# A retention and low-rank mixer kernel on one core: three of batch 0's v loads issued by GpSimd's queue, and the first batch's ramp in another order

## The chip, the cores and the metric

The kernel runs on one core of one Trainium2 chip. The metric is the device time of one execution in microseconds. A core has five engines that run side by side, each with its own queue of instructions, which it works off strictly in order: TensorE (PE in the profile, its weight loads PEld), VectorE (DVE), ScalarE (ACT), GpSimd (POOL) and SyncE (SP). They wait for one another through semaphores. Transfers between the chip's memory and the core's are issued from an engine's queue and then run by themselves; in this kernel SP issues most of them, and GpSimd those of the weights.

## The reference, cut to what matters

Batch, heads, tokens and head size are 4, 8, 768 and 64, so a token has 512 channels; the hidden size is 2048 and the rank 32.

```python
state = gamma * state + k_t (outer) v_t        # per head, gamma = 1 - 2^(-5-h)
y_t   = scale * q_t @ state                    # 768 tokens in order
x     = y laid out as (batch, 768, 512)
u     = x + (x^T @ U @ V)^T                    # low rank, over the tokens
out   = u + relu(u @ w_ch1) @ w_ch2
```

The kernel does the recurrence in six chunks of 128 tokens: inside a chunk by a masked product of q and k, across chunks by a state that goes on from chunk to chunk.

## The kernel before

The work is one long stream of matmuls, batch after batch. While a batch's MLP runs, the retention of the next batch is put in between the MLP's matmuls by a table (`PLANS`): each entry gives the number of the MLP slot ahead of which a step of the next batch stands. A slot is one group of MLP matmuls. Nothing is scheduled by the machine: the order in which the Python code calls the steps is the order in each engine's queue.

Batch 0 has no MLP ahead of it. Its retention, its low-rank part and the first load of weights are the *ramp*, and its order is written out by hand: a list of pairs of function and arguments, which a loop calls one after another. The change is in this list. The functions it names, all for batch 0:

- `run_idle(n, bank)`: n matmuls on zeros that only keep TensorE busy.
- `qd(i, e, engine)` and `kd(c, engine)`: scale half e of q's pair i (chunks 2i and 2i+1, whose tokens alternate between the halves), or k of chunk c, by the decay, into tile `qk`. G is GpSimd, V is DVE, A is ACT.
- `turn_q`, `turn_k`: four matmuls each with the identity, which transpose them; `evict_q`, `evict_k` copy the result from PSUM to `q0T` and `kT`.
- `scores(c)`, `keep(c, e)`: the products of q and k, and DVE's masking of them into tile `a`.
- `cast_v(c, engine)`: v to bf16 (`vb`). Chunk 5's is done in two halves.
- `sums(c)`, `state(c, engine)`: the sum of k and v over the chunks so far, in one PSUM bank, and its copy `st`, block by block. `sums` of a chunk writes to the bank that `state` of the chunk before read.
- `inter(c)`, `intra(c)`, `evict_x(c)`: the output of chunk c from the earlier chunks' state and from its own scores, and its copy `x`. Chunk 5 is done in two halves.
- `turn_x`, `low`, `evict_P`, `high`, `evict_u`: x transposed, the low-rank products and the eviction of their sum u to `uT`, which the MLP reads. `spread_V`, `evict_V` spread the matrix V.
- `load_w1(lo, w)`: a load of w columns of the first weight, issued by GpSimd.

Input tiles are loaded by `load_pair` (two chunks in 512 KB, into tile `in`) and `load_one` (one chunk in 256 KB, into `k_n` or `v_n`). SP's queue issues them at the program's start in this order: q of pair 0, k of chunks 0 and 1, q of pair 1, k 2, k 3, v of chunks 0 and 1, q of pair 2, k 4, v 2, k 5, v 3, v 4, v 5. In the order listings `DMA v_n_2 ... 128x8x64` is the load of v of chunk 2: 128 tokens, 8 heads, 64 elements.

Of the kernel before, what the change touches and what calls it, by code (L numbers as in the profile page):

```python
# [47 lines left out]
def kernel(  # L48
# [80 lines left out]

    gate = (1, 0)  # L130

    def load_one(t, b, c, src, nm):
# [3 lines left out]
        nc.sync.dma_start(out=n, in_=src[b, :, ts(c, P), :].rearrange("h p d -> p h d"))
# [181 lines left out]

    def kd(c, eng):
        t = qk_of(c)[:, 1]  # L320
        i, g = (in0[:, 0, :, c], Gk0) if c < 2 else (t0["k_n", c], Gk)
        eng.tensor_tensor(t, i, g[:, c].unsqueeze(2).to_broadcast([P, H, D]), op=ALU.mult)
# [488 lines left out]
    for f, *args in (
        (run_idle, 6, 5), (qd, 0, 1, V), (kd, 2, G), (run_idle, 11, 5), (qd, 0, 0, V), (qd, 1, 0, G),
        (kd, 0, V), (turn_k, 0), (turn_q, 0, 1), (turn_q, 0, 0), (kd, 1, V), (evict_k, 0, V),
        (evict_q, 0, 0, A), (run_idle, 1, 5), (evict_q, 0, 1, A), (turn_k, 1), (evict_k, 1, A),
        (scores, 1), (qd, 1, 1, V), (keep, 1, 0), (run_idle, 2, 2), (kd, 3, G), (scores, 0),
        (turn_q, 1, 1), (keep, 1, 1), (spread_V, 1), (turn_q, 1, 0), (evict_q, 1, 1, A), (keep, 0, 0),
        (evict_q, 1, 0, A), (keep, 0, 1), (cast_v, 1, V), (turn_k, 2), (qd, 2, 1, G), (evict_k, 2, A),
        (cast_v, 0, A), (spread_V, 0), (scores, 2), (kd, 4, G), (run_idle, 1, 1), (evict_V, 1, V),
        (keep, 2, 0), (turn_k, 3), (evict_V, 0, A), (sums, 0), (kd, 5, G), (evict_k, 3, A), (intra, 0),
        (state, 0, A), (keep, 2, 1), (scores, 3), (sums, 1), (qd, 2, 0, V), (run_idle, 1, 1),  # L820
        (keep, 3, 1), (load_w1, 0, 256), (evict_x, 0, A), (turn_q, 2, 1), (inter, 1), (state, 1, A),
        (keep, 3, 0), (turn_q, 2, 0), (turn_k, 4), (evict_q, 2, 1, A), (evict_k, 4, V), (intra, 1),
        (evict_q, 2, 0, A), (cast_v, 2, V), (scores, 4), (evict_x, 1, A), (sums, 2), (inter, 2),
        (intra, 2), (run_idle, 1, 0), (keep, 4, 1), (state, 2, A), (cast_v, 3, V),
        (load_w1, DH // 2, 256), (keep, 4, 0), (inter, 3), (turn_k, 5), (evict_x, 2, A), (intra, 3),
        (turn_x, 0, 0), (sums, 3), (evict_k, 5, A), (turn_x, 0, 2), (cast_v, 5, G, 0), (state, 3, V),
        (turn_x, 0, 1), (scores, 5), (cast_v, 5, G, 1), (cast_v, 4, A), (keep, 5, 0), (evict_x, 3, A),
        (sums, 4), (state, 4, A), (inter, 4), (intra, 4), (low, (0, 1, 2, 3)), (keep, 5, 1),
        (load_w1, 256, 768), (inter, 5, 0), (inter, 5, 1), (evict_x, 4, A), (intra, 5, 1),
        (intra, 5, 0), (turn_x, 0, 3), (evict_x, 5, V, 1), (low, (4,)), (evict_x, 5, A, 0),  # L830
        (low, (5,)), (turn_x, 1, 1), (turn_x, 1, 2), (evict_P, 0, A), (evict_P, 1, A), (turn_x, 1, 0),
        (high, 0, 0), (high, 0, 1), (high, 0, 3), (high, 1, 2), (evict_u, 0, 1, V), (high, 0, 2),
        (evict_u, 0, 3, A), (high, 1, 1), (high, 1, 0), (evict_u, 1, 2, V), (turn_x, 1, 3),
        (load_w1, DH // 2 + 256, 256), (evict_u, 0, 0, A), (high, 1, 3), (evict_u, 1, 0, V),
        (evict_u, 0, 2, A), (evict_u, 1, 1, V), (evict_u, 1, 3, A),
    ):
# [3 lines left out]
    PLANS = (  # L840
        {
            "in": [38, 41, 42, 46, 49, 52],
            "v": [47, 49, 57, 55, 58, 63],
            "T": [45, 49, 51, 54, 55, 63],
            "S": [((0,), 47), ((1,), 52), ((2,), 55), ((3,), 58), ((4,), 62), ((5,), 65)],
            "O": [49, 54, 57, 60, 64, 68],
            "load": [],
            "P": 69,
# [14 lines left out]
        {
            "in": [1, 8, 13, 14, 20, 23],
            "v": [27, 28, 33, 43, 39, 45],
            "T": [3, 13, 18, 18, 21, 26],
            "S": [((0, 1), 27), ((2,), 35), ((3,), 42), ((4,), 44), ((5,), 47)],
            "O": [31, 37, 43, 45, 50, 52],
            "load": [(3, 3, 0), (3, 4, 11), (3, 5, 14)],
            "P": 54,  # L870
            "n": [(0, 56), (1, 56), (2, 56), (3, 59), (4, 59), (5, 59)],
            "u": [],
        },
    )
# [1 line left out]
    for b in range(B):  # L876
        nxt = b + 1 < B
        slots = mlp1_slots(b)
        n1 = len(slots)
        side = {}  # L880
        set_banks([0, 1, 2, SA, SB, OB])
        if b == 0:
            taken.update({i: n for n, i in enumerate((1, 2, 0, OB, SA, SB, TP))})
# [9 lines left out]
            for j, i in enumerate([0, 5, 12, 14, 19, 24]):  # L893
# [1 line left out]
            for i, f, *args in ((8, g_sums, 0, 0, 2), (18, g_sums, 0, 2, 2), (23, w2_sum, 0, range(4)),
                                (26, g_sums, 0, 4, 2), (24, w2_sum, 1, (0,)), (28, w2_sum, 1, (1,)),
                                (33, g_sums, 0, 6, 1, range(3)), (32, w2_sum, 1, (2,)),
                                (33, g_sums, 0, 7, 1, range(3)), (33, hold_pool),
                                (39, w2_sum, 1, (3,)), (33, g_sums, 0, 6, 2, (3,))):
# [1 line left out]
            put(side, n1 + 22, flush)
        if b == 1:
            put(side, 21, flush)
# [1 line left out]
            for j, i in enumerate([9, 0, 4]):
                put(side, i, lambda j=j: mix_r(1, j))
        if b:
            for m0, w, i in zip((0, 2, 4, 6, 7), (2, 2, 2, 1, 1), [[12, 20, 25, 30, 32], [12, 16, 25, 28, 32], [12, 20, 25, 29, 32]][b - 1]):
# [54 lines left out]
```

## Time and profile before

| what | us |
|---|---|
| runs shown | 223.07, 223.14, 222.38; median 223.07 |
| the profiled execution, its own time | 222.57 |
| its span, first to last instruction | 220.8 |
| TensorE busy | 211.3 |
| DVE, ACT, GpSimd busy | 146.1, 121.4, 77.7 |
| first matmul of batch 0's MLP | 29.47 |

A row of the timeline reads: start, duration, engine, line, operation, what it writes `<-` what it reads, shape, count, and in brackets the idle time of the engine before it with what ended it. `SPq` is an issue of a transfer in SP's queue. A row on a transfer gives its count, its size and the median time from the issue's start to the landing. Most matmuls are recorded by one helper and so carry one line, L116; they are told apart by the tiles that they read: `<-q0T,kT` are scores, `<-vb,qk` sums, `<-st,q0T` inter, `<-vb,a` intra, `<-ident,qk` turns of q or k, `<-ident,x` turn_x, `<-x,Ub` low, `<-Vb,P_sb` high, `<-uT,w1b` the MLP.

### The profile page before, as it was taken

The numbers are of one execution on the slowest core, as the hardware profiler recorded it, in microseconds if no ns is written. First come the engines' busy times: TensorE is split into PE (matmuls) and PEld (weight loads), VectorE is DVE, ScalarE is ACT, GpSimd is POOL, SyncE is SP. The second block draws the span as 40 slices with busy tenths as digits, with TensorE's granted clock in tenths as the row PEclk, the third lists the DMA queues.
The fourth block names the chain that finished last, engine by engine and source line by source line (L and its number), as shares of the span: only waits on it lengthen the run. The fifth ranks groups of instructions, "written<-read, shape, count | busy, mean of one in ns | idle before, by whom it ended". The sixth has DMA issues, their size and how long they took to land.

```text
span 220.8 us, 5024 instructions
## 1 busy us (share of the span) xinstructions
PE 211.3 (96%) x1999; PEld 154.8 (70%) x2002; DVE 146.1 (66%) x293; ACT 121.4 (55%) x252; POOL 77.7 (35%) x89
## 2 busy tenths in 40 slices
PE   7868999999999999999999999999999999999993
PEld 2447755668888765667887876666887866668883
DVE  7678566798887872579974720889885602566662
ACT  3268856775147466777444737777444557771000
POOL 5075820004986501904243279550423430000000
PEclk9999999999999999999999999999999999999999
DMA  6999999999999968999999389999020570000222
GB/s 164 241 268 180 141 200 214 213 222 221 202 215 181 228 172 164 190 204 299 203 199 219 73 146 225 229 227 155 3 95 3 129 198 11 0 0 0 98 95 97
DMA packets 98583, 34.89 MB, mean 158 GB/s; under 512 B 86752, under 2 KB 94848, under 8 KB 98560
## 3 DMA queue, kind: packets, MB, share of 16 engines
q1 hardware_dynamic: 94112, 30.02, 66.5%
q0 software_dynamic: 4304, 4.29, 12.1%
q8 instruction: 15, 0.25, 0.5%
q10 hardware_dynamic: 144, 0.26, 0.3%
q14 instruction: 8, 0.07, 0.1%
HBM read 27.46 MB, written 6.29 MB: 153 GB/s over the span
## 4 chain that ended last, share of the span: by engine, by line
PE 88%; DVE 5%; ACT 4%; issue 1%; DVEq 0%; ACTq 0%
PE bk L116 86%; ACT st L310 1%; DVE a L463 1%; PE bk L440 1%; ACT q0T L310 1%; DVE gs L621 1%; DVE a L368 1%; ACT kT L310 1%; ACT P_sb L121 1%; DVE res L697 0%; DVE st L400 0%; PE bk L334 0%; ACT gT L121 0%; DVE Vb L312 0%; PE bk L346 0%
## 5 line engine op out<-in xcount | busy, mean ns | idle before, releaser
L116 PE MATMUL bk<-uT,w1b 128*128 128x384 bf16 x512 | 85.9, 326 | 0.0
L116 PEld LDWEIGHTS <-w1b 128*128 128x128 bf16 x512 | 53.7, 106 | 29.6 <-issue 0.4
L121 ACT ACTIVATE gT<-bk 128x384 bf16<-128x384 f32 x125 | 61.1, 490 | 23.8 <-PE bk L116 23.0
L697 DVE TENSOR_TENSOR res<-bk,res 128x256 f32<-128x256 f32 (+2 forms) x66 | 30.3, 462 | 21.3 <-PE bk L116 20.3
L116 PEld LDWEIGHTS <-gT 128*128 128x128 bf16 x384 | 36.3, 98 | 7.4 <-issue 1.8
L116 PE MATMUL bk<-w2b,gT 128*128 128x256 bf16 x288 | 37.6, 273 | 0.0
L116 PEld LDWEIGHTS <-gs 128*128 128x128 bf16 x296 | 27.5, 98 | 4.0
L268 POOL TENSOR_TENSOR qk<-k_n,Gk 128x512 bf16<-128x512 f32 x18 | 19.8, 1102 | 25.8 <-DMA k_n<-in_k_dram 19.2
L621 DVE TENSOR_TENSOR gs<-gT 128x768 bf16<-128x768 bf16 (+1 forms) x20 | 10.6, 532 | 27.4 <-ACT gT L121 27.4
L116 PE MATMUL bk<-w2s,gs 128*128 128x256 bf16 x192 | 25.7, 273 | 0.0
L463 DVE TENSOR_TENSOR a<-bk,mask 128x512 bf16<-128x512 f32 x36 | 22.9, 681 | 1.2 <-PE bk L116 1.0
L562 DVE TENSOR_TENSOR res<-bk,x 128x512 f32<-128x512 f32 x24 | 15.9, 687 | 9.3 <-PE bk L116 7.9
L697 POOL TENSOR_TENSOR res<-s,res 128x512 f32<-128x512 f32 (+2 forms) x13 | 13.7, 1059 | 22.6 <-DVE res L697 17.1
L480 ACT ACTIVATE x<-bk 128x512 bf16<-128x512 f32 x18 | 10.8, 598 | 18.7 <-PE bk L116 16.4
L273 POOL TENSOR_TENSOR qk<-q_n,Gq 128x512 bf16<-128x512 f32 x18 | 19.7, 1096 | 0.4 <-DMA q_n<-in_q_dram 0.2
L697 POOL TENSOR_TENSOR res<-c,res 128x256 f32<-128x256 f32 x12 | 8.7, 725 | 16.4 <-ACT c L692 16.4
L279 ACT ACTIVATE vb<-v_n 128x512 bf16<-128x512 f32 x18 | 11.0, 624 | 4.6 <-DMA v_n<-in_v_dram 4.5
L116 PE MATMUL bk<-w2b,gs 128*128 128x256 bf16 (+1 forms) x104 | 13.1, 265 | 0.0
L116 PE MATMUL bk<-w2s,gT 128*128 128x256 bf16 x96 | 13.1, 273 | 0.0
L621 DVE TENSOR_TENSOR gT<-gT 128x768 bf16<-128x768 bf16 (+1 forms) x20 | 12.0, 598 | 0.0
L567 ACT ACTIVATE x<-res 128x512 bf16<-128x512 f32 x15 | 9.1, 629 | 4.5 <-DVE res L562 4.5
L621 DVE TENSOR_TENSOR gs<-gs,gT 128x768 bf16<-128x768 bf16 (+1 forms) x20 | 11.1, 553 | 0.7
(98 smaller groups left out, 218.3 us busy)
## 6 DMA issues: line engine op xcount, KB each, us to landing
k_n<-in_k_dram SPq DMA_DIRECT2D x22, 256.0 KB, 4.8
v_n<-in_v_dram SPq DMA_DIRECT2D x22, 256.0 KB, 5.0
out_dram<-res SPq DMA_DIRECT2D x22, 256.0 KB, 2.5
q_n<-in_q_dram SPq DMA_DIRECT2D x18, 256.0 KB, 4.9
w2b<-in_moe_w_ch_dram POOLq DMA_DIRECT2D x4, 512.0 KB, 14.7
in<-in_q_dram SPq DMA_DIRECT2D x3, 512.0 KB, 6.2
w1b<-in_moe_w_ch_dram POOLq DMA_DIRECT2D x3, 256.0 KB, 6.1
...
```

The source lines that it names most:

```text
L116: nc.tensor.matmul(o, l, r, **kw)
L121: nc.scalar.activation(o, i, AF.Relu if relu else AF.Copy)
L268: eng.tensor_tensor(kd, k_n, Gk[:, c].unsqueeze(2).to_broadcast([P, H, D]), op=ALU.mult)
L273: eng.tensor_tensor(qd, rc[b, c]["q_n"], Gq[:, c].unsqueeze(2).to_broadcast([P, H, D]), op=ALU.mult)
L279: nc.scalar.activation(vb, rc[b, c]["v_n"], AF.Copy)
L310: nc.scalar.activation(o, i, AF.Copy)
L463: nc.vector.tensor_tensor(r["a"][:, e], r["s"][e].rearrange("p (n t) -> p n t", n=NP), mask4, op=ALU.mult)
L480: nc.scalar.activation(x_of(b, c), o, AF.Copy)
L562: nc.vector.tensor_tensor(res_of(b, j), h, xs[b, j], op=ALU.add)
L567: nc.scalar.activation(xs[b, j], res_of(b, j), AF.Copy)
L621: nc.vector.tensor_tensor(o, x, y, op=op)
L697: eng.tensor_tensor(x, y, x, op=ALU.add)
```

## The change

Three loads, v of chunks 2, 4 and 5, leave SP's queue. They are now issued by GpSimd's, from the middle of the ramp, by a new function `load_late`. Of SP's list there remains k 5 directly behind k 4, and then v 3. The ramp's list has another order, with other engines for some steps: q and k of pair 0 and q of pair 1 are divided between DVE and GpSimd, q's turns come ahead of k's, k 1 ahead of k 0. There are 20 idle matmuls in the list instead of 23. The two wide w1 loads of the ramp stand at its end. In `PLANS` and in the tables of side steps some slots are moved, mostly by one to three.

```diff
-    def load_one(t, b, c, src, nm):
+    def load_one(t, b, c, src, nm, eng=nc.sync):
...
-        nc.sync.dma_start(out=n, in_=src[b, :, ts(c, P), :].rearrange("h p d -> p h d"))
+        eng.dma_start(out=n, in_=src[b, :, ts(c, P), :].rearrange("h p d -> p h d"))
...
-    for what in ("q0", "kA", "q1", "k2", "k3", "vA", "q2", "k4", "v2", "k5", "v3", "v4", "v5"):
+    for what in ("q0", "kA", "q1", "k2", "k3", "vA", "q2", "k4", "k5", "v3"):
...
+    def load_late(nm, c, eng):
+        load_one(t0, 0, c, {"k": k, "v": v}[nm], nm + "_n", eng)
...
-        (run_idle, 6, 5), (qd, 0, 1, V), (kd, 2, G), (run_idle, 11, 5), (qd, 0, 0, V), (qd, 1, 0, G),
-        (kd, 0, V), (turn_k, 0), (turn_q, 0, 1), (turn_q, 0, 0), (kd, 1, V), (evict_k, 0, V),
...
+        (qd, 0, 0, V), (qd, 0, 1, G), (run_idle, 9, 5), (turn_q, 0, 1), (turn_q, 0, 0), (kd, 1, V),
+        (evict_q, 0, 0, A), (run_idle, 4, 5), (turn_k, 1), (evict_k, 1, A), (kd, 0, G),
...
+        (keep, 1, 0), (kd, 3, G), (load_late, "v", 2, G), (load_late, "v", 4, G),
+        (load_late, "v", 5, G), (keep, 1, 1), (evict_q, 1, 0, A), (turn_q, 1, 1),
...
-            "load": [(3, 0, 26), (3, 1, 42), (3, 2, 40), (2, 3, 4), (2, 4, 8), (2, 5, 17)],
+            "load": [(3, 0, 29), (3, 1, 43), (3, 2, 38), (2, 3, 5), (2, 4, 8), (2, 5, 17)],
```

GpSimd's queue from its first scaling to the first loads of the first weight, before:

```order
L322 TENSOR_TENSOR qk_2_201<-k_n_2_101,Gk 128x512
L327 TENSOR_TENSOR qk_2_201<-in_97,Gq_168 128x512
L322 TENSOR_TENSOR qk_3_267<-k_n_3_103,Gk 128x512
L327 TENSOR_TENSOR qk_5_317<-in_97,Gq_168 128x512
L322 TENSOR_TENSOR qk_4_336<-k_n_4_107,Gk 128x512
L322 TENSOR_TENSOR qk_5_317<-k_n_5_111,Gk 128x512
L161 DMA w1b_403<-in_moe_w_ch_dram 128x4x256
L161 DMA w1b_489<-in_moe_w_ch_dram 128x4x256
```

The same place of the changed kernel:

```order
L330 TENSOR_TENSOR qk_1_188<-in_97,Gq_162 128x512
L325 TENSOR_TENSOR qk_0_186<-in_97,Gk_164 128x512
L330 TENSOR_TENSOR qk_2_254<-in_97,Gq_162 128x512
L325 TENSOR_TENSOR qk_2_254<-k_n_2_101,Gk 128x512
L325 TENSOR_TENSOR qk_3_252<-k_n_3_103,Gk 128x512
L136 DMA v_n_2_287<-in_v_dram 128x8x64
L136 DMA v_n_4_289<-in_v_dram 128x8x64
L136 DMA v_n_5_291<-in_v_dram 128x8x64
L330 TENSOR_TENSOR qk_5_303<-in_97,Gq_162 128x512
L325 TENSOR_TENSOR qk_4_328<-k_n_4_107,Gk 128x512
L325 TENSOR_TENSOR qk_5_303<-k_n_5_109,Gk 128x512
L161 DMA w1b_428<-in_moe_w_ch_dram 128x4x256
```

Two scalings of pair 0 came in at the front, and the three loads of v stand between k of chunk 3 and q of chunk 5.

DVE's queue from the second masking of chunk 2 to v of chunk 2, before:

```order
L368 TENSOR_TENSOR a_2_327<-bk_20_326,mask 128x512
L327 TENSOR_TENSOR qk_4_336<-in_97,Gq_168 128x512
L368 TENSOR_TENSOR a_3_382<-bk_26_381,mask 128x512
L368 TENSOR_TENSOR a_3_382<-bk_25_380,mask 128x512
L312 COPY kT_4_431<-bk_31_425 128x512
L312 CAST vb_2_450<-v_n_2_109 128x512
L368 TENSOR_TENSOR a_4_454<-bk_33_453,mask 128x512
```

The same place of the changed kernel, from the masking of chunk 2's second half on, and on to the state of chunk 3:

```order
L371 TENSOR_TENSOR a_2_332<-bk_22_331,mask 128x512
L330 TENSOR_TENSOR qk_4_328<-in_97,Gq_162 128x512
L371 TENSOR_TENSOR a_3_381<-bk_26_379,mask 128x512
L371 TENSOR_TENSOR a_3_381<-bk_27_380,mask 128x512
L312 CAST x_1_443<-bk_28_400 128x512
L312 COPY kT_4_445<-bk_30_432 128x512
L312 CAST vb_2_455<-v_n_2_287 128x512
L371 TENSOR_TENSOR a_4_466<-bk_35_465,mask 128x512
L312 CAST vb_3_504<-v_n_3_111 128x512
L371 TENSOR_TENSOR a_4_466<-bk_34_464,mask 128x512
L403 TENSOR_TENSOR st_179<-bk_24_349,bmask 128x512
```

The output x of chunk 1 is now copied by DVE and stands ahead of k of chunk 4, and v of chunk 3 is cast between the two maskings of chunk 4.

More of the change, by code (lines that the diff above doesn't have):

```diff
@@ L817 @@
[L817 to L833, printed above, removed]
@@ L834 @@
-        (load_w1, DH // 2 + 256, 256), (evict_u, 0, 0, A), (high, 1, 3), (evict_u, 1, 0, V),
-        (evict_u, 0, 2, A), (evict_u, 1, 1, V), (evict_u, 1, 3, A),
+        (qd, 0, 0, V), (qd, 0, 1, G), (run_idle, 9, 5), (turn_q, 0, 1), (turn_q, 0, 0), (kd, 1, V),
+        (evict_q, 0, 0, A), (run_idle, 4, 5), (turn_k, 1), (evict_k, 1, A), (kd, 0, G),
+        (turn_k, 0), (evict_q, 0, 1, V), (run_idle, 1, 5), (scores, 1), (qd, 1, 1, V),
+        (qd, 1, 0, G), (run_idle, 1, 2), (turn_q, 1, 0), (evict_k, 0, A), (scores, 0), (kd, 2, G),
@@ new lines @@
+        (keep, 1, 0), (kd, 3, G), (load_late, "v", 2, G), (load_late, "v", 4, G),
+        (load_late, "v", 5, G), (keep, 1, 1), (evict_q, 1, 0, A), (turn_q, 1, 1),
+        (evict_q, 1, 1, A), (keep, 0, 1), (keep, 0, 0), (qd, 2, 1, G), (spread_V, 0),
+        (spread_V, 1), (evict_V, 1, A), (turn_k, 2), (evict_k, 2, V), (run_idle, 2, 1),
+        (turn_k, 3), (evict_k, 3, V), (evict_V, 0, A), (kd, 4, G), (scores, 2), (cast_v, 1, V),
+        (kd, 5, G), (cast_v, 0, A), (run_idle, 2, 1), (sums, 0), (keep, 2, 0), (state, 0, A),
@@ new lines @@
+        (intra, 0), (keep, 2, 1), (scores, 3), (evict_x, 0, A), (sums, 1), (inter, 1), (intra, 1),
+        (qd, 2, 0, V), (turn_q, 2, 1), (keep, 3, 0), (load_w1, 0, 256), (load_w1, DH // 2, 256),
+        (turn_k, 4), (turn_q, 2, 0), (keep, 3, 1), (evict_x, 1, V), (evict_k, 4, V), (state, 1, A),
+        (inter, 2), (evict_q, 2, 1, A), (cast_v, 2, V), (run_idle, 1, 0), (sums, 2),
+        (evict_q, 2, 0, A), (scores, 4), (intra, 2), (state, 2, A), (inter, 3), (evict_x, 2, A),
+        (turn_k, 5), (keep, 4, 1), (evict_k, 5, A), (turn_x, 0, 0), (cast_v, 3, V), (sums, 3),
@@ new lines @@
+        (keep, 4, 0), (intra, 3), (scores, 5), (turn_x, 0, 2), (state, 3, V), (cast_v, 4, A),
+        (keep, 5, 1), (evict_x, 3, A), (sums, 4), (state, 4, A), (keep, 5, 0), (inter, 4),
+        (intra, 4), (low, (0, 1, 2, 3)), (inter, 5, 1), (cast_v, 5, G, 1), (cast_v, 5, G, 0),
+        (intra, 5, 1), (evict_x, 5, V, 1), (evict_x, 4, A), (inter, 5, 0), (intra, 5, 0),
+        (turn_x, 0, 3), (turn_x, 0, 1), (low, (4,)), (evict_x, 5, A, 0), (low, (5,)),
+        (evict_P, 0, A), (turn_x, 1, 1), (turn_x, 1, 2), (turn_x, 1, 0), (evict_P, 1, A),
@@ L836 @@
+        (high, 0, 0), (high, 0, 1), (evict_u, 0, 0, V), (evict_u, 0, 1, V), (high, 1, 0),
+        (evict_u, 1, 0, A), (high, 0, 2), (turn_x, 1, 3), (high, 1, 2), (high, 0, 3),
+        (evict_u, 0, 2, V), (evict_u, 0, 3, V), (high, 1, 1), (evict_u, 1, 1, V), (high, 1, 3),
+        (evict_u, 1, 3, A), (evict_u, 1, 2, V), (load_w1, 256, 768),
+        (load_w1, DH // 2 + 256, 256),
     ):
@@ L841 @@
         {
[L842 to L843 removed]
+            "in": [38, 41, 44, 47, 52, 54],
+            "v": [47, 49, 56, 56, 59, 64],
             "T": [45, 49, 51, 54, 55, 63],
[L845 removed]
+            "S": [((0,), 47), ((1,), 52), ((2,), 55), ((3,), 57), ((4,), 62), ((5,), 65)],
             "O": [49, 54, 57, 60, 64, 68],
@@ L864 @@
             "in": [1, 8, 13, 14, 20, 23],
[L865 to L869, printed above, removed]
+            "v": [25, 28, 35, 40, 35, 41],
+            "T": [3, 12, 18, 16, 20, 26],
+            "S": [((0, 1), 27), ((2,), 37), ((3,), 42), ((4,), 45), ((5,), 47)],
+            "O": [32, 37, 43, 45, 50, 53],
+            "load": [(3, 3, 1), (3, 4, 9), (3, 5, 12)],
             "P": 54,
-            "n": [(0, 56), (1, 56), (2, 56), (3, 59), (4, 59), (5, 59)],
+            "n": [(0, 57), (1, 56), (2, 56), (3, 59), (4, 59), (5, 59)],
             "u": [],
@@ L892 @@
                 put(side, 14, lambda c=c, nm=nm: load_chunk(1, c, nm))
[L893 removed]
+            for j, i in enumerate([0, 5, 13, 15, 16, 24]):
                 put(side, i, lambda j=j: mix_r(0, j))
[L895 removed]
+            for i, f, *args in ((9, g_sums, 0, 0, 2), (17, g_sums, 0, 2, 2), (23, w2_sum, 0, range(4)),
                                 (26, g_sums, 0, 4, 2), (24, w2_sum, 1, (0,)), (28, w2_sum, 1, (1,)),
[L897 removed]
+                                (31, g_sums, 0, 6, 1, range(3)), (32, w2_sum, 1, (2,)),
                                 (33, g_sums, 0, 7, 1, range(3)), (33, hold_pool),
[L899 removed]
+                                (38, w2_sum, 1, (3,)), (34, g_sums, 0, 6, 2, (3,))):
                 put(side, i, lambda f=f, args=args: f(*args))
[L901 removed]
+            put(side, n1 + 23, flush)
         if b == 1:
[L903 removed]
+            put(side, 24, flush)
             slots[:2] = [lambda: mlp1_two(1, (0, HM), 0), lambda: None]
[L905 removed]
+            for j, i in enumerate([8, 0, 3]):
                 put(side, i, lambda j=j: mix_r(1, j))
         if b:
[L908 removed]
+            for m0, w, i in zip((0, 2, 4, 6, 7), (2, 2, 2, 1, 1), [[12, 22, 25, 30, 32], [12, 16, 25, 28, 33], [12, 20, 25, 28, 32]][b - 1]):
                 put(side, i, lambda m0=m0, w=w: g_sums(b, m0, w))
```

11 lines of the change are left out of this document (4 added, 7 removed).

## The prediction

> **What bounds the kernel now.** I read the page first, then the busy time by stretch, then the waits of TensorE, and last the rows of the ramp engine by engine.
>
> ```profile
> span 220.8 us, 5024 instructions
> PE 211.3 (96%) x1999; PEld 154.8 (70%) x2002; DVE 146.1 (66%) x293; ACT 121.4 (55%) x252; POOL 77.7 (35%) x89
> PE 88%; DVE 5%; ACT 4%; issue 1%; DVEq 0%; ACTq 0%
> ...
> 10.00:15.00 5.00, 2.84 (x51) 1.51 (x49) 3.31 (x7) 3.01 (x6) 3.04 (x3) 1.00 1.19 267
> 15.00:20.00 5.00, 4.35 (x84) 3.57 (x85) 4.53 (x7) 4.68 (x11) 2.08 (x2) 1.00 1.14 191
> 20.00:25.00 5.00, 3.93 (x81) 3.43 (x79) 3.39 (x8) 4.13 (x10) 3.84 (x6) 1.00 0.95 164
> 29.47:40.00 10.53, 10.53 (x65) 6.26 (x64) 6.38 (x12) 6.65 (x17) 0.00 (x0) 1.00 1.21 210
> ...
> PE bk L116 <- DVE a L463: 0.3, 1, 0.3
> ```
>
> TensorE is busy 96% of the span, and the chain that ended last is 88% TensorE. In the rows by stretch (first PE, then PEld, DVE, ACT, POOL, granted clock, DMA share, GB/s) it has no hole from 29.47 on; the last line is the only wait that the trace shows behind that point. So what stands behind 29.47, where the first matmul of batch 0's MLP begins, moves as a block: the change is worth what it moves that matmul by. In the ramp before it TensorE waits, and its turns are these:
>
> ```profile
> 11.63 0.42 PE L116 MATMUL bk<-q0T,kT 64*64 64x128 bf16 x16 [1.42 <-ACT kT L310]
> 19.27 0.39 PE L334 MATMUL bk<-ident,qk 128*128 128x128 bf16 x4
> 19.59 0.64 PE L116 MATMUL bk<-vb,a 64*128 64x64 bf16 x16
> 20.98 0.40 PE L116 MATMUL bk<-vb,qk 128*128 128x128 bf16 x4
> 23.16 0.39 PE L116 MATMUL bk<-vb,qk 128*128 128x128 bf16 x4
> 26.57 0.59 PE L116 MATMUL bk<-x,Ub 128*32 128x512 bf16 x2
> 29.47 3.41 PE L116 MATMUL bk<-uT,w1b 128*128 128x384 bf16 x20
> ```
>
> In the names of the table these are scores of chunk 1, turn_k 4, intra 1, sums 2, sums 3, low 4 and 5, and the first MLP slot. From sums 3 to the end of low 5 is 23.16 to 27.16, 4.0 us: the states of chunks 3 and 4 and the output of chunk 5 follow one another there. From low 5 to the MLP is 2.3 us more.
>
> The loads feed this:
>
> ```profile
> 11.83 1.68 SPq L136 DMA_DIRECT2D v_n<-in_v_dram  x1
> 13.55 1.85 SPq L136 DMA_DIRECT2D k_n<-in_k_dram  x1
> 15.45 4.76 SPq L136 DMA_DIRECT2D v_n<-in_v_dram  x3
> ...
> 16.00:18.00 2.00, 1.76 (x40) 1.50 (x39) 2.00 (x3) 1.79 (x5) 1.81 (x2) 1.00 1.33 223
> 18.00:20.00 2.00, 2.00 (x39) 1.69 (x37) 2.00 (x4) 1.89 (x5) 0.00 (x0) 1.00 0.84 142
> 20.00:22.00 2.00, 1.41 (x32) 1.21 (x30) 1.36 (x4) 1.54 (x5) 1.45 (x2) 1.00 0.84 189
> 22.00:24.00 2.00, 1.69 (x35) 1.57 (x36) 1.03 (x3) 1.90 (x5) 1.39 (x3) 1.00 0.89 136
> ...
> v_n<-in_v_dram SPq DMA_DIRECT2D x1, 256.0 KB, 7.6
> k_n<-in_k_dram SPq DMA_DIRECT2D x1, 256.0 KB, 6.9
> ...
> 20.55 1.04 POOL L322 TENSOR_TENSOR qk<-k_n,Gk 128x512 bf16<-128x512 f32 x1 [2.60 <-DMA k_n<-in_k_dram]
> 23.77 0.74 POOL L312 CAST vb<-v_n 128x256 bf16<-128x256 f32 x2 [0.61 <-DMA v_n<-in_v_dram]
> ```
>
> SP's queue issues v of chunk 2 at 11.83 (lands 7.6 later, 19.4), k of 5 at 13.55 (6.9 later, 20.45), then v of 3, 4 and 5; the three take 4.76 us to issue. GpSimd waits 2.60 us for k of 5, and v of 5 ends its wait at 23.77. The last column shows the transfers at 223 GB/s up to 18 and at 142, 189 and 136 after it: SP's issuing, not the transfer rate, thins out the last loads.
>
> **The change part by part.**
>
> *Front of the ramp.* Before, DVE made both q of pair 0 and both k; now each pair is divided between DVE and GpSimd, q is turned first, and k of chunk 1 ahead of k of 0. Prices of one scaling:
>
> ```profile
> 7.50 1.29 DVE L322 TENSOR_TENSOR qk<-in,Gk 128x512 bf16<-128x512 f32 x2 [0.80 <-DMA in<-in_k_dram]
> 17.05 1.46 DVE L327 TENSOR_TENSOR qk<-in,Gq 128x512 bf16<-128x512 f32 x1
> ...
> 16.92 1.04 POOL L322 TENSOR_TENSOR qk<-k_n,Gk 128x512 bf16<-128x512 f32 x1
> ```
>
> A DVE scaling is 0.65, but 1.46 where it starts beside one of GpSimd's (17.05 against 16.92). So I take the pairs as one behind the other: k of 1 is ready at 8.2 if DVE is first, at 9.0 if GpSimd is. Its turn (about 0.4 with the hand-over) and its eviction (0.6) put scores 1 at 9.3 to 10.3 instead of 11.63: 1.3 to 2.3 us ahead. Three idle matmuls fewer cost and save nothing, since they fill waits. That lead runs down to intra 1 (about 17.5 for 19.59), but behind it the PE queue holds turn_k 4 and sums 2, which hang on GpSimd and on loads. So the front alone is costed at nothing; if the loads came earlier, it would show.
>
> *GpSimd's queue.* It gains three issues between k of 3 and q of 5, and two scalings at the front. The price of an issue of 1024 pieces (128x8x64) is not in the trace from this engine. Nearest rows:
>
> ```profile
> 1.41 0.70 POOL L209 DMA_DIRECT2D Vs<-in_moe_V_dram  x1
> 2.10 0.88 POOL L210 DMA_DIRECT2D Ub<-in_moe_U_dram  x1
> ```
>
> Vs is 32 rows in 0.70, Ub 768 pieces (128x6x32) in 0.88; drawn on to 1024 that is 0.95, my value. Lower end 0.70; upper end SP's 1.68 for the same load. K of 3 ended before at about 14.1 behind two other scalings; one of these (1.03) is gone from ahead of it, so the issues start at 13.0 to 13.5. Three of 0.95 end at 16.2; q of 5 then ends at 17.2 and k of 4 at 18.3, so turn_k 4 comes at 18.4 against 19.27. The cover here is 0.9 us. At more than 1.25 us an issue it is used up.
>
> *The loads.* SP's order is the same up to k of 4. Then k of 5 has the place of v 2 (19.4, before 20.45) and v of 3 that of k 5 (20.45, before 21.55). GpSimd's loads run beside them:
>
> ```profile
> Vs<-in_moe_V_dram POOLq DMA_DIRECT2D x1, 48.0 KB, 5.7
> Ub<-in_moe_U_dram POOLq DMA_DIRECT2D x1, 48.0 KB, 6.6
> w1b<-in_moe_w_ch_dram POOLq DMA_DIRECT2D x2, 256.0 KB, 6.1
> v_n<-in_v_dram SPq DMA_DIRECT2D x1, 256.0 KB, 4.5
> ```
>
> From that queue, beside SP's traffic, 5.7 to 6.6 us pass to landing. V of 2, issued at 13.3, lands at 19.0 to 19.9 (before 19.4): no loss, no gain. V of 4 and 5 follow at 20.5 to 21.9, before 22.8 (by its place) and 23.7. The three take 768 KB of transfer time from SP's last two loads: at 223 GB/s 1.1 us for each 256 KB, of which I charge one to v of 3. So it lands at 21.5, as before, and k of 5 at 19.4 to 20.4.
>
> [...]
>
> *The path to the end.* V of 2 cast (0.42) at 19.5 to 20.4 lets sums 2 run at about 20.1, before 20.98. Then the state of 2 (0.78) to 21.1, inter 3, turn_k 5, the first turn_x (0.65 together) to 21.75. V of 3, landed at 21.5 and cast, lets sums 3 run at 22.0; before 23.16.
>
> ```profile
> 24.86 0.78 ACT L310 ACTIVATE st<-bk 64x256 bf16<-64x256 f32 x2 [0.31 <-PE bk L116]
> 14.49 0.42 DVE L312 CAST vb<-in 128x512 bf16<-128x512 f32 x1
> ```
>
> The 4.0 us behind sums 3 hold the same states, casts and outputs in nearly the same order; DVE's state of 3 now stands behind keep 4, so I add 0.15. Low 5 ends at 26.15 against 27.16: 1.0 us gained. The end of the ramp then has the same three turns, eight high products and one more turn; four of the first evictions on DVE feed the first MLP slot, which needs only two of them at its start. Costed at nothing; the other order of evictions could cost or give 0.2.
>
> *Weights and later slots.* The first two w1 loads are issued when k of 5 is done, about 20.5 (before 21.54, 6.1 to landing): at the MLP by 27. The 768 wide load stands behind the cast of v 5, which is earlier too. The moved slots of batches 1 and 2 lie where TensorE has work queued: nothing, with 0.4 us either way as bounds, from the one 0.3 us wait.
>
> Sum: 1.0 us. The profiled execution took 222.57 (span 220.8 and 1.8 around it), so 221.6; the median of the runs is 0.5 above it, and 223.07 less 1.0 is 222.1.
>
> **The rivals.**
>
> *The lead of the front is kept* (0.20). If GpSimd's loads land in 4.5 us, as the last v_n does, v of 2 is there at 17.8, and sums 2 waits only for turn_k 4 and chunk 1's output, 19.2. The gain is 1.8: 221.3. For it: that row had little traffic beside it. Against: at 13 to 18 the DMA share is over 1.
>
> *The loads are no earlier* (0.20). If the shared engines give GpSimd's loads their turn ahead of SP's, v of 3 is last, up to 22.6 (20.45 and two times 1.1), sums 3 runs at 23.1, and nothing is gained: 223.0. For it: same bytes, same engines. Against: the thin stretch from 18 to 24, which the earlier issues fill.
>
> *GpSimd becomes the bound* (0.16). If an issue takes 1.68, as SP's does, three end at 18.3 and turn_k 4 comes at 20.6 instead of 19.27; its scores and all behind them are 1.3 later: 224.4. It decides from 1.25 us an issue. For it: SP needs 1.68 for the same load. Against: Ub's 0.88 with three quarters of the pieces. One more thing speaks for it: DVE and GpSimd hold each other up (1.46 above), and DVE runs two kT copies and a cast (0.42 each) in that stretch; all on the issues, that is 1.37 each and 0.35 lost against before, 223.4. [...]
>
> **How the numbers follow.** My forecast, a gain of 0.5 to 1.5, has 0.44: about 222.1, own range 221.5 to 222.6. Half a per cent, what a measurement of this kernel can tell from no change, is 1.1 us: faster means under 221.95, slower over 224.2. The forecast gives 0.22 to faster and 0.22 to same; the kept lead 0.20 to faster; loads no earlier 0.20 to same; GpSimd as bound 0.13 to slower and 0.03 to same. Faster 0.42, same 0.45, slower 0.13. The range reaches from the kept lead with 0.4 of moved slots (220.9) to an issue between 1.37 and 1.68 (223.8); it leaves out about 0.1 on each side.
>
> **What the profile after would show.** Scores 1 near 10; three GpSimd issues of about 0.95 from 13.3; q of 5 ending near 17.2; GB/s from 18 to 22 over 200; v of 5 cast before 23; sums 3 near 22.0; the first MLP matmul near 28.5. Wrong it would be through an issue over 1.25 us, through v of 2 or 3 landing after 20.5 or 22, or through new TensorE waits behind 29.

## The result and the profile after

The changed kernel takes 224.79 us (median of 5 runs, 223.75 to 225.27) against 223.07 (222.37 to 223.14): a ratio of 1.0084, interval 1.0058 to 1.0109. It is 1.7 us slower. The prediction said 222.1 with a range of 220.9 to 223.8, so it was wrong in sign and outside its range. The profiled execution took 224.53, with a span of 222.8.

The page of the changed kernel: the span, the busy times, the granted clock in 40 slices, and the chain that ended last.

```profile
span 222.8 us, 5024 instructions
PE 213.4 (96%) x1999; PEld 156.2 (70%) x1999; DVE 146.3 (66%) x295; ACT 119.9 (54%) x248; POOL 84.5 (38%) x94
PEclk9998599999999999999999999999999999999999
PE bk L116 82%; DMA v_n<-in_v_dram 5%; SPq L136 3%; SPq L176 2%; DVE gs L624 2%; PE bk L443 1%; DVE a L466 1%; ACT P_sb L121 1%; DVE state L511 0%; DVE vb L312 0%; ACT gT L121 0%; DVE res L700 0%; DVE gT L624 0%
```

The number of TensorE instructions is unchanged and it is again busy 96%, but in the fifth slice (22.3 to 27.8 us) it was granted half its clock, and a transfer of v now stands in the chain with 5%. The stretches say where (columns as before: PE, PEld, DVE, ACT, POOL, granted clock, DMA share, GB/s):

```profile
15.00:20.00 5.00, 3.93 (x71) 2.96 (x69) 3.48 (x6) 3.59 (x7) 3.74 (x4) 1.00 1.21 222
20.00:22.00 2.00, 1.05 (x12) 0.65 (x11) 0.43 (x1) 0.37 (x1) 1.96 (x3) 0.75 0.89 174
22.00:24.00 2.00, 1.79 (x21) 1.63 (x20) 0.70 (x2) 1.47 (x4) 0.19 (x1) 0.50 1.23 156
24.00:26.00 2.00, 1.46 (x20) 1.19 (x19) 1.77 (x3) 1.03 (x3) 2.00 (x4) 0.50 0.84 110
26.00:28.00 2.00, 2.00 (x25) 1.73 (x23) 1.29 (x2) 1.10 (x4) 2.00 (x4) 0.54 0.97 97
```

From 20 to 22 TensorE runs 12 matmuls where it ran 32 before. From 26 to 28 it is busy all the time and still does only 25, at a clock of 0.54. Its turns, from the timeline (scores of chunk 1, intra 1, turn_k 4, sums 2, sums 3, low, the first MLP slot):

```profile
9.69 0.42 PE L116 MATMUL bk<-q0T,kT 64*64 64x128 bf16 x16
16.95 0.64 PE L116 MATMUL bk<-vb,a 64*128 64x64 bf16 x16
18.13 0.40 PE L337 MATMUL bk<-ident,qk 128*128 128x128 bf16 x4 [0.21 <-POOL qk L325]
20.95 0.57 PE L116 MATMUL bk<-vb,qk 128*128 128x128 bf16 x4 [1.77 <-DVE vb L312]
24.54 0.58 PE L116 MATMUL bk<-vb,qk 128*128 128x128 bf16 x4 [0.75 <-DVE vb L312]
28.98 0.58 PE L116 MATMUL bk<-x,Ub 128*32 128x512 bf16 x2
31.73 2.44 PE L116 MATMUL bk<-uT,w1b 128*128 128x384 bf16 x14
```

Scores 1 are 1.9 us earlier than before and intra 1 is 2.6 earlier. The whole lead is spent at sums 2 (20.95 for 20.98), which waits 1.77 us for the cast of v 2. Sums 3 are then 1.4 us late, and the MLP starts at 31.73 instead of 29.47. The loads behind it, with the two casts on DVE and the one on GpSimd, and the last, from the chain of work, the load that sums 3 hang on:

```profile
12.98 2.74 POOL L136 DMA_DIRECT2D v_n<-in_v_dram  x3
13.32 1.86 SPq L136 DMA_DIRECT2D v_n<-in_v_dram  x1
20.47 0.43 DVE L312 CAST vb<-v_n 128x512 bf16<-128x512 f32 x1 [1.49 <-DMA v_n<-in_v_dram]
23.99 0.49 DVE L312 CAST vb<-v_n 128x512 bf16<-128x512 f32 x1 [1.17 <-DMA v_n<-in_v_dram]
23.81 0.93 POOL L312 CAST vb<-v_n 128x256 bf16<-128x256 f32 x2 [1.85 <-DMA v_n<-in_v_dram]
...
13.32 10.65 DMA v_n<-in_v_dram
```

GpSimd issued its three loads in 2.74 us, 0.91 each. V of chunk 2 lands at 20.45, 7.5 after its issue. V of 3, which SP issued at 13.32 as its last load of the ramp, needs 10.65 us and lands at 23.97. V of 5 is cast at 23.81, as in the kernel before (23.77): issued some 4 us earlier, it is there no earlier.

What the two queues moved meanwhile (packets, MB, share of the 16 engines; `q0 software_dynamic` is GpSimd's queue, `q1 hardware_dynamic` SP's), from 17.5 to 19, from 19 to 20.5 and from 20.5 to 24:

```profile
q0 software_dynamic: 93, 0.32, 99.6%
q1 hardware_dynamic: 51, 0.01, 5.5%
...
q1 hardware_dynamic: 966, 0.24, 103.8%
q0 software_dynamic: 35, 0.08, 24.9%
...
q0 software_dynamic: 675, 0.51, 98.1%
q1 hardware_dynamic: 71, 0.02, 3.2%
```

From 17.5 to 19 SP's queue nearly stands still: 0.01 MB against 0.32. A record of GpSimd's queue is 3.4 KB on average there (0.32 MB by 93), one of SP's is a single piece of 256 bytes (0.24 MB by 966 from 19 to 20.5); from 16 to 17.5 GpSimd's are 4.1 KB each (0.18 MB by 44). From 19 to 20.5 it is the other way round. K of 5 is there by then (its scaling starts at 19.31), so these 966 pieces are nearly all of v 3's 1024. The last 71 pass only between 20.5 and 24, beside v 5 and the weights that GpSimd issues from 20.3 on: at the end v 3 waits for these few.

By what rule the records of the two queues follow one another the rows do not show.

### The profile page after: what moved, and what is told of

Same layout as the page of the kernel before. It is cut to its first block, busy times and chain, and to the rows that moved or that the text cites. A ratio compares the mean times of both kernels' runs of the same rounds, so it can differ in the third digit from the quotient of the medians.

```text
span 222.8 us, 5024 instructions
## 1 busy us (share of the span) xinstructions
PE 213.4 (96%) x1999; PEld 156.2 (70%) x1999; DVE 146.3 (66%) x295; ACT 119.9 (54%) x248; POOL 84.5 (38%) x94
## 4 chain that ended last, share of the span: by engine, by line
PE 83%; SPq 5%; DMA 5%; DVE 4%; issue 1%; ACT 1%
PE bk L116 82%; DMA v_n<-in_v_dram 5%; SPq L136 3%; SPq L176 2%; DVE gs L624 2%; PE bk L443 1%; DVE a L466 1%; ACT P_sb L121 1%; DVE state L511 0%; DVE vb L312 0%; ACT gT L121 0%; DVE res L700 0%; DVE gT L624 0%
## 5 line engine op out<-in xcount | busy, mean ns | idle before, releaser
L121 ACT ACTIVATE gT<-bk 128x384 bf16<-128x384 f32 x125 | 61.1, 490 | 23.5 <-PE bk L116 23.3
L116 PEld LDWEIGHTS <-gs 128*128 128x128 bf16 x296 | 27.8, 98 | 4.4 <-DVE gs L624 0.8
L268 POOL TENSOR_TENSOR qk<-k_n,Gk 128x512 bf16<-128x512 f32 x18 | 19.9, 1103 | 25.3 <-DMA k_n<-in_k_dram 17.6
L700 POOL TENSOR_TENSOR res<-s,res 128x512 f32<-128x512 f32 (+2 forms) x13 | 13.7, 1060 | 21.6 <-DVE res L700 16.2
L273 POOL TENSOR_TENSOR qk<-q_n,Gq 128x512 bf16<-128x512 f32 x18 | 19.9, 1105 | 0.1
L624 DVE TENSOR_TENSOR gs<-gs,gT 128x768 bf16<-128x768 bf16 (+1 forms) x20 | 11.7, 587 | 0.7
```

The lines of the kernel that those rows point to most:

```text
L116: nc.tensor.matmul(o, l, r, **kw)
L121: nc.scalar.activation(o, i, AF.Relu if relu else AF.Copy)
L268: eng.tensor_tensor(kd, k_n, Gk[:, c].unsqueeze(2).to_broadcast([P, H, D]), op=ALU.mult)
L273: eng.tensor_tensor(qd, rc[b, c]["q_n"], Gq[:, c].unsqueeze(2).to_broadcast([P, H, D]), op=ALU.mult)
L624: nc.vector.tensor_tensor(o, x, y, op=op)
L700: eng.tensor_tensor(x, y, x, op=ALU.add)
```

## The experiments

The first theory (theory 1) was that the loss lies in the loads: GpSimd's, in records of 4 KB, take the engines from SP's, in records of 256 bytes, v 2 and v 3 come late, and TensorE's idle time then costs it its clock. The rivals were that the new order is itself slower (theory 2), and that the moved slots are (theory 3). In the later experiments the rival of theory 1 is that any second queue does the harm, whatever its records.

**The order without the loads.** All loads in SP's queue again, in the old order; ramp and slots as changed.

```diff
-    for what in ("q0", "kA", "q1", "k2", "k3", "vA", "q2", "k4", "k5", "v3"):
+    for what in ("q0", "kA", "q1", "k2", "k3", "vA", "q2", "k4", "v2", "k5", "v3", "v4", "v5"):
...
-        (keep, 1, 0), (kd, 3, G), (load_late, "v", 2, G), (load_late, "v", 4, G),
-        (load_late, "v", 5, G), (keep, 1, 1), (evict_q, 1, 0, A), (turn_q, 1, 1),
+        (keep, 1, 0), (kd, 3, G), (keep, 1, 1), (evict_q, 1, 0, A), (turn_q, 1, 1),
```

> The changed order and slots, but all 13 loads issued by SP in the order of before. [...] Without GpSimd's loads v 2 lands at about 19.4 and v 3 at 21.5 as before, the granted clock stays at 1.00 from 20 to 28, the first MLP matmul comes at 28.3 to 29.3, and the time is 221.8 to 222.9. Theory 2 (the order): the new order itself leaves TensorE idle and costs the clock; then the MLP starts after 31 and the time stays at 224 to 225. Theory 3 (the moved slots): the ramp is faster but the time stays over 223.5.

Measured: 220.99 (220.83 to 221.38), ratio 0.9923, interval 0.9900 to 0.9947. Its sums 2, its sums 3, its first MLP slot, the cast of v 3, and the stretch from 20 to 22:

```profile
19.53 0.38 PE L116 MATMUL bk<-vb,qk 128*128 128x128 bf16 x4 [0.40 <-DVE vb L312]
21.77 0.38 PE L116 MATMUL bk<-vb,qk 128*128 128x128 bf16 x4
27.95 3.41 PE L116 MATMUL bk<-uT,w1b 128*128 128x384 bf16 x20
...
21.29 0.43 DVE L312 CAST vb<-v_n 128x512 bf16<-128x512 f32 x1 [0.28 <-DMA v_n<-in_v_dram]
...
20.00:22.00 2.00, 1.66 (x32) 1.28 (x29) 1.41 (x3) 1.61 (x4) 1.79 (x2) 1.00 0.97 217
```

The new order gains 2.1 us by itself (1.6 between the two profiled executions), with the granted clock at 1.00 in every stretch from 6 to 40 us. The time lies below the 221.8 to 222.9 of theory 1, and the MLP starts earlier than it said. So the three loads cost 3.8 us (224.79 less 220.99). This kernel is faster than both.

**The loads without the order.** Old ramp and old slots; SP's short list, and the three loads in GpSimd's queue behind k of 3.

```diff
-            (scores, 1), (qd, 1, 1, V), (keep, 1, 0), (run_idle, 2, 2), (kd, 3, G), (scores, 0),
+            (scores, 1), (qd, 1, 1, V), (keep, 1, 0), (run_idle, 2, 2), (kd, 3, G), (load_late, "v", 2, G),
+            (load_late, "v", 4, G), (load_late, "v", 5, G), (scores, 0),
```

> The order and slots of before; only the three v loads are issued by GpSimd, behind k of chunk 3. Theory 1: v 3 lands at 23 to 24.5 here too instead of 21.55, sums 3 runs 1 to 2 us later than 23.16, and the time is 224 to 225.5. Theories 2 and 3: the loads cost nothing, 222.5 to 223.3.

Measured: 224.51 (222.72 to 225.27), ratio 1.0061, interval 1.0026 to 1.0095. The time is as expected, the way there is not. V of 3 took 8.2 us from its issue at 13.42 and was there by 21.6, with the same three loads beside it. DVE's scaling of q of chunk 4 and what waited for it:

```profile
17.97 2.60 DVE L330 TENSOR_TENSOR qk<-in,Gq 128x512 bf16<-128x512 f32 x1
17.95 2.06 POOL L325 TENSOR_TENSOR qk<-k_n,Gk 128x512 bf16<-128x512 f32 x2
20.62 0.55 PE L349 MATMUL bk<-ident,qk 128*128 128x128 bf16 x4 [0.94 <-DVE qk L330]
...
20.00:22.00 2.00, 1.38 (x14) 1.38 (x15) 1.77 (x3) 0.91 (x2) 1.49 (x3) 0.68 0.97 176
22.00:24.00 2.00, 2.00 (x32) 1.61 (x30) 0.88 (x3) 1.29 (x2) 0.20 (x1) 0.50 1.34 179
```

The issues pushed GpSimd's two scalings of k back until they fell together with DVE's of q, which took 2.60 us instead of 1.46. That the one lengthened the other is read from the two rows, and no run tests it. TensorE waited, and its clock fell here too. The two runs whose clock was 0.997 and 0.998 took 222.72 and 223.61, the four at 0.990 to 0.992 took 224.38 to 225.27. On the old order the loads cost 1.4 us, on the new one 3.8. The two parts don't add up: only the new order brings TensorE to sums 2 before v 2 is there.

**The moved slots.** The changed kernel with the old numbers in `PLANS` and the tables of side steps, for example:

```diff
-            "in": [0, 4, 13, 10, 21, 24],
-            "v": [26, 27, 32, 45, 49, 52],
...
+            "in": [0, 4, 13, 7, 22, 25],
+            "v": [29, 29, 34, 45, 49, 53],
...
```

> The changed ramp and loads, with the tables of slots (PLANS and the side steps) of before. Theories 1 and 2: the ramp costs all of it, so the time stays at 224.3 to 225.2. Theory 3: it falls to 223.3 or less. Here 0.3 us either way would be the slots' own worth.

Measured: 224.78 (224.36 to 225.28), ratio 1.0092, interval 1.0063 to 1.0120. The slots are worth nothing that these runs can tell.

**The clock's share.** Nine idle matmuls instead of one ahead of sums 2, where TensorE waits in any case.

```diff
-        (inter, 2), (evict_q, 2, 1, A), (cast_v, 2, V), (run_idle, 1, 0), (sums, 2),
+        (inter, 2), (evict_q, 2, 1, A), (cast_v, 2, V), (run_idle, 9, 0), (sums, 2),
```

> The changed kernel with 9 idle matmuls instead of 1 ahead of sums 2, where TensorE waits 1.77 us for v 2. The loads are as late as in the changed kernel. If the halved clock (21.6 to 28.4) is a consequence of that wait, the clock stays at 1.00, the waits for v 2 and v 3 stay, the MLP starts near 30.3 instead of 31.7, and the time is 223.2 to 223.8. If the clock falls for another reason, or its fall is beside the path, the time stays at 224.5 to 225.

Measured: 223.22 (222.52 to 224.76), ratio 1.0015, interval 0.9992 to 1.0037.

```profile
20.00:22.00 2.00, 1.99 (x25) 1.09 (x24) 0.65 (x2) 0.50 (x2) 2.00 (x3) 1.00 0.82 162
22.00:24.00 2.00, 0.90 (x13) 0.66 (x11) 0.46 (x1) 1.90 (x4) 0.14 (x1) 1.00 1.12 146
24.59 0.38 PE L116 MATMUL bk<-vb,qk 128*128 128x128 bf16 x4 [1.43 <-DVE vb L312]
30.76 3.41 PE L116 MATMUL bk<-uT,w1b 128*128 128x384 bf16 x20
```

The clock stays at 1.00, and sums 3 are still at 24.59, since v 3 lands as late as before. From sums 3 to the first MLP slot it is 6.17 us here, 7.19 in the changed kernel and 6.31 in the kernel before. So the halved clock costs 1.57 us by the medians (224.79 less 223.22) and 0.85 by the two profiled executions (224.53 and 223.68). The late loads cost the other 2.2 of the 3.8, or 2.7 by the profiled executions.

The granted clock of each run is on record and says the same inside single kernels. Of the next experiment's ten runs the five at 1.00 took 221.34 to 222.11, and the three at 0.981 to 0.985 took 223.43 to 223.84. With v of 2 alone by GpSimd three runs at 0.999 or 1.00 took 221.40 to 221.97, and seven at 0.990 to 0.992 took 222.50 to 223.07. Here nine of ten runs were at 0.999 or 1.00, and the slowest, 224.76, at 0.992.

The rows give the length of a fall: 6.8 us at half clock in the changed kernel (1.0 of the stretch from 20 to 22, 4.0 from 22 to 26, 1.8 from 26 to 28), and 3.4 in the next experiment, whose clock was 0.68 from 18 to 20, 0.50 from 20 to 22 and 0.97 from 22 to 24. What sets a fall off they leave open: in the 3.4 us ahead of the fall at 21.0 TensorE was busy for 1.42, and in the next experiment for 2.7 of the 3.4 ahead of a fall at 18.7. With the idle fill a wait of 1.43 us ahead of sums 3 passed without a fall; in the changed kernel one of 1.77, in a stretch with other gaps, came with one.

**All four v by GpSimd.** V of 3 leaves SP's queue too and stands second in GpSimd's.

```diff
-    for what in ("q0", "kA", "q1", "k2", "k3", "vA", "q2", "k4", "k5", "v3"):
+    for what in ("q0", "kA", "q1", "k2", "k3", "vA", "q2", "k4", "k5"):
...
-        (keep, 1, 0), (kd, 3, G), (load_late, "v", 2, G), (load_late, "v", 4, G),
-        (load_late, "v", 5, G), (keep, 1, 1), (evict_q, 1, 0, A), (turn_q, 1, 1),
+        (keep, 1, 0), (kd, 3, G), (load_late, "v", 2, G), (load_late, "v", 3, G),
+        (load_late, "v", 4, G), (load_late, "v", 5, G), (keep, 1, 1), (evict_q, 1, 0, A), (turn_q, 1, 1),
```

> The changed kernel with v of chunk 3 issued by GpSimd's queue too, second of four (v 2, 3, 4, 5); SP ends with k 5. [...] V 2 stays at about 20.4, so the wait at sums 2 stays and the clock may still fall; sums 3 runs at 22 to 22.7 instead of 24.5, time 222.8 to 224. Rival (the core takes any second queue badly, whatever the packets): v 3 still lands after 23, time 224.3 or more.

Measured: 222.17 (221.34 to 223.84), ratio 0.9980, interval 0.9953 to 1.0007. The cast of v 3 and sums 3:

```profile
22.70 0.42 DVE L312 CAST vb<-v_n 128x512 bf16<-128x512 f32 x1
23.17 0.39 PE L116 MATMUL bk<-vb,qk 128*128 128x128 bf16 x4
```

The cast no longer waits, and sums 3 are 1.4 us earlier than in the changed kernel, although one more load goes by GpSimd. V of 3 lands at 21.6, not after 23 as by the rival, and the time is below the 222.8 to 224 expected. What delayed v 3 was its place, alone in SP's queue beside three loads of GpSimd's.

**V of 2 alone by GpSimd.** V of 3, 4 and 5 stay in SP's queue.

```diff
-    for what in ("q0", "kA", "q1", "k2", "k3", "vA", "q2", "k4", "k5", "v3"):
+    for what in ("q0", "kA", "q1", "k2", "k3", "vA", "q2", "k4", "k5", "v3", "v4", "v5"):
...
-        (keep, 1, 0), (kd, 3, G), (load_late, "v", 2, G), (load_late, "v", 4, G),
-        (load_late, "v", 5, G), (keep, 1, 1), (evict_q, 1, 0, A), (turn_q, 1, 1),
+        (keep, 1, 0), (kd, 3, G), (load_late, "v", 2, G), (keep, 1, 1), (evict_q, 1, 0, A), (turn_q, 1, 1),
```

> The changed order; only v of chunk 2 is issued by GpSimd at the changed place, SP issues k 4, k 5, v 3, v 4, v 5. Theory 1: v 2's 64 packets pass ahead of SP's, 1.1 us of transfer, so v 2 lands at about 19.5 to 20.4 and v 3 at about 21 to 22, since no more of GpSimd's packets stand against it until the first weight at 22.5; the clock is 1.00 or falls shortly, time 221.3 to 222.8. Rival (any second queue): as bad as the changed kernel, 224 or more.

Measured: 222.71 (221.40 to 223.07), ratio 0.9984, interval 0.9962 to 1.0006.

```profile
12.97 0.95 POOL L136 DMA_DIRECT2D v_n<-in_v_dram  x1
20.32 0.43 DVE L312 CAST vb<-v_n 128x512 bf16<-128x512 f32 x1 [1.35 <-DMA v_n<-in_v_dram]
PE bk L116 <- DVE vb L312: 1.5, 1, 1.5
```

V of 2 alone in GpSimd's queue is as late (20.3) as with two loads behind it, and costs 1.7 us against the order alone, part of it through the clock, which fell to 0.50 from 22 to 24. SP issued this load at 11.49 in the order alone and its cast began at 19.05; GpSimd issues it at 12.97, behind the scaling of k 3. It takes 7.5 us to land in the one and 7.3 in the other, so what makes it late is the later issue. V of 3, with one load of GpSimd's beside it, landed at 21.4.

**Only the late pair by GpSimd.** V of 2 back in SP's list ahead of k 5, and v 4 and 5 issued behind k of 4.

```diff
-    for what in ("q0", "kA", "q1", "k2", "k3", "vA", "q2", "k4", "k5", "v3"):
+    for what in ("q0", "kA", "q1", "k2", "k3", "vA", "q2", "k4", "v2", "k5", "v3"):
...
-        (keep, 1, 0), (kd, 3, G), (load_late, "v", 2, G), (load_late, "v", 4, G),
-        (load_late, "v", 5, G), (keep, 1, 1), (evict_q, 1, 0, A), (turn_q, 1, 1),
+        (keep, 1, 0), (kd, 3, G), (keep, 1, 1), (evict_q, 1, 0, A), (turn_q, 1, 1),
...
-        (turn_k, 3), (evict_k, 3, V), (evict_V, 0, A), (kd, 4, G), (scores, 2), (cast_v, 1, V),
+        (turn_k, 3), (evict_k, 3, V), (evict_V, 0, A), (kd, 4, G), (load_late, "v", 4, G), (load_late, "v", 5, G), (scores, 2), (cast_v, 1, V),
```

> The changed order; SP issues k 4, v 2, k 5, v 3 as in before's order, GpSimd issues only v 4 and v 5, behind k of chunk 4 (about 17 to 18). Theory 1: their packets start at about 21, when v 2 and k 5 have landed; v 2 at 19.4 and v 3 at 21.5 as with SP alone, v 4 and 5 by 23.5, clock 1.00, time 220.7 to 221.5, like the order alone (220.99). If v 3 is not done when they start, it is starved: v 3 after 22.5, time 221.8 to 223.

Measured: 221.25 (221.01 to 221.37), ratio 0.9924, interval 0.9894 to 0.9953.

```profile
17.89 1.85 POOL L136 DMA_DIRECT2D v_n<-in_v_dram  x2
19.32 0.38 PE L116 MATMUL bk<-vb,qk 128*128 128x128 bf16 x4 [0.26 <-DVE vb L312]
21.55 0.38 PE L116 MATMUL bk<-vb,qk 128*128 128x128 bf16 x4
```

With SP's v 2 and v 3 ahead of them, GpSimd's loads harm nothing, and they bring nothing: the time can't be told from the order alone.

**Loads that cast on the way.** The same three loads write bf16 straight into `vb`; the casts of v 2, 4 and 5 are gone.

```diff
-        load_one(t0, 0, c, {"k": k, "v": v}[nm], nm + "_n", eng)
+        r0["v", c] = rmid.tile([P, H, D], bf16, tag="vb", name=f"vb_0_{c}", bufs=6)
+        eng.dma_start(out=r0["v", c], in_=v[0, :, ts(c, P), :].rearrange("h p d -> p h d"))
...
-        (inter, 2), (evict_q, 2, 1, A), (cast_v, 2, V), (run_idle, 1, 0), (sums, 2),
+        (inter, 2), (evict_q, 2, 1, A), (run_idle, 1, 0), (sums, 2),
...
```

> The changed kernel, but GpSimd's three loads write bf16 straight into the tiles that cast_v filled, so their packets are 128 bytes on the written side and no cast of v 2, 4, 5 remains. [...] Clock 1.00 or a short fall, time 221.3 to 223. Rival (any second queue): v 3 still after 23, time over 224.

Measured: 221.44 (220.94 to 221.53), ratio 0.9932, interval 0.9905 to 0.9959. The queues from 17 to 18:

```profile
q0 software_dynamic: 1129, 0.14, 223.8%
q1 hardware_dynamic: 51, 0.01, 10.4%
```

The records of GpSimd's queue are small now (0.14 MB in 1129, 128 bytes each), but the two queues do not share evenly: 22 of them pass for each one of SP's. SP's loads are held back here too, with records of 128 bytes as with those of 4 KB; v 3 landed at 21.97. The gain over the changed kernel is therefore no proof that the size of the records decides: v 2 needs no cast, three casts less run on the ramp's engines, and the clock did not fall.

**The same loads by ScalarE's queue.**

```diff
-        (keep, 1, 0), (kd, 3, G), (load_late, "v", 2, G), (load_late, "v", 4, G),
-        (load_late, "v", 5, G), (keep, 1, 1), (evict_q, 1, 0, A), (turn_q, 1, 1),
+        (keep, 1, 0), (kd, 3, G), (load_late, "v", 2, A), (load_late, "v", 4, A),
+        (load_late, "v", 5, A), (keep, 1, 1), (evict_q, 1, 0, A), (turn_q, 1, 1),
```

> The changed kernel with the three loads of v 2, 4 and 5 issued by ScalarE's queue, at the place in its order right behind the eviction of k of 0, and not by GpSimd's. [...] Rival (any second queue takes the bandwidth from SP's): v of 3 again lands more than 10 us after its issue, at 23.5 or later. [...]

Measured: 223.00 (222.37 to 224.97), ratio 1.0024, interval 0.9993 to 1.0055. The queues from 16 to 16.5 (`q10` is ScalarE's), the landing of k 5, SP's queue from 22 to 23.8, SP's issues, and the cast of v 3:

```profile
q10 hardware_dynamic: 471, 0.12, 128.1%
q1 hardware_dynamic: 13, 0.00, 4.1%
...
k_n<-in_k_dram SPq DMA_DIRECT2D x1, 256.0 KB, 11.0
...
q1 hardware_dynamic: 71, 0.02, 5.1%
...
10.37 4.14 SPq L136 DMA_DIRECT2D k_n<-in_k_dram  x2
14.56 2.77 SPq L136 DMA_DIRECT2D v_n<-in_v_dram  x1
23.77 0.43 DVE L312 CAST vb<-v_n 128x512 bf16<-128x512 f32 x1 [0.75 <-DMA v_n<-in_v_dram]
```

Over the stretch from 15 to 17 the two queues look even (0.28 MB for SP's, 0.24 for ScalarE's), but they do not share: from 15 to 15.5 only SP's moves, from 16 to 16.5 ScalarE's moves 471 pieces and SP's 13. All these records are single pieces (0.12 MB by 471, about 256 bytes), so neither their size nor GpSimd's queue is needed for one queue to hold up the other. The rival is borne out in k 5, which took 11.0 us from its issue at 11.78, where it took 7.7 in the changed kernel. V of 3 took 9.2 us and landed at 23.8, past the rival's 23.5, though not over 10 us. SP's issues themselves took longer (4.14 and 2.77 us, for 3.00 and 1.86), so it went out 1.24 later. Here too its last 71 pieces came late, from 22 on, though no other transfer was under way then. Why they lag is not shown in either kernel.

**The landings side by side.** In the traces of these runs the last five input loads land one behind the other, whichever queue issues them (us of the landing):

| | first | second | third | fourth | fifth |
|---|---|---|---|---|---|
| kernel before | v 2 19.4 | k 5 20.5 | v 3 21.6 | v 4 22.7 | v 5 23.7 |
| order alone | v 2 19.0 | k 5 20.1 | v 3 21.3 | v 4 22.4 | v 5 23.3 |
| v of 2 alone by GpSimd | k 5 19.1 | v 2 20.3 | v 3 21.4 | v 4 22.5 | v 5 23.5 |
| all four v by GpSimd | k 5 19.2 | v 2 20.4 | v 3 21.6 | v 4 22.7 | v 5 23.7 |
| changed kernel | k 5 19.2 | v 2 20.5 | v 4 21.6 | v 5 23.8 | v 3 24.0 |

The places lie about 1.1 us apart and are taken in the order in which the issues end. The one exception is v 3 of the changed kernel: its issue ends at 15.18, ahead of v 5's at 15.72, so its place was the fourth, at about 22.7 by the other rows (an estimate). So v 2 lost one place to k 5, and v 3 one to v 4 and another 1.3 us with its last pieces.

## Why the prediction was wrong

What it got right, by its own steps: what stands behind the first MLP matmul moves as a block (that matmul 2.26 us later, the execution 1.96). Scores 1 came at 9.69, inside 9.3 to 10.3. The issues took 0.91 each for 0.95, with two copies (0.92 together) and a cast (0.42) of DVE's beside them, and started at 12.98; q of 5 ended at 17.07 for 17.2, turn_k 4 ran at 18.13 for 18.4, intra 1 at 16.95 for 17.5. GpSimd was not the bound, and k of 5, scaled from 19.31, was inside 19.4 to 20.4 but for 0.1. The moved slots are nothing.

The step that failed is v of 3: "at 223 GB/s 1.1 us for each 256 KB, of which I charge one to v of 3. So it lands at 21.5". It landed at 23.97, 2.5 later, which is more than two further loads at that price. Of three loads' transfer time I charged one to v 3 and gave no reason for leaving out the others. The price held, for the places of the table lie 1.1 us apart. But the issues of two of the three, v 2 and v 4, ended ahead of v 3's own, which by the table puts it at 22.7; the other 1.3 us are its last pieces, beside v 5 and the weights. A landing after 22 was among the signs of being wrong that I had named. The rival "the loads are no earlier" charged two loads: v 3 at 22.6, no gain, 223.0. It was right in kind and short by 1.4 us of landing. Its argument against, the thin stretch that earlier issues fill, held only in part: from 18 to 20 the rate was 202 GB/s for 142, but from 20 to 22 it was 174, below the 189 of before, and v 5 was there no sooner. That SP's issuing thins out the last loads, as I read that stretch, is not what the end of the ramp hung on: the late pair by GpSimd gave nothing.

The smaller miss is v of 2, at 20.45 where 19.0 to 19.9 was forecast; sums 2 came at 20.95 for 20.1. Its issue moved from SP's 11.83 to 12.98, and from GpSimd's queue it took 7.5 us, beyond the 6.6 of the slowest row that I had used. A nearer row stood among those I quote: the same load in SP's queue took 7.6.

"So the front alone is costed at nothing" failed too, by the 2.1 us of the order alone; in its profile sums 3 come 1.4 earlier (21.77 for 23.16). My reason was that turn_k 4 and sums 2 hang on loads. But the quoted rows had the answer: v 2 landed at 19.4 and its cast takes 0.42, so it could be ready at 19.8, and sums 2 ran only at 20.98; v 3 was there at 21.5 and sums 3 ran at 23.16. The loads had over a microsecond of slack, and the order was the limit. With the loads left where they were, the numbers of the rival "the lead of the front is kept" came out: sums 2 at 19.5 for its 19.2, and 220.99 for its 221.3. That is luck as far as its condition goes, for it had GpSimd's loads landing within 4.5 us, and in the changed kernel they took 7.5 to 8.9.

The clock was not in the sum at all. I treated a wait of TensorE as costing its length; here it also halved the clock for the 6.8 us that followed, 0.9 to 1.6 us by the idle fill. The idle matmuls ahead of sums 2, which I costed with all others as fillers, were one, where nine were enough.

Sum by the runs: order −2.1, late loads +2.2, clock +1.6, slots 0; together +1.7. The parts are differences of one chain of medians, so they must add up to what was measured; by the profiled executions they are −1.6, +2.7 and +0.9, together +2.0.
